# First chunk of an mLSTM cell with a SwiGLU block: how k and q are turned, which engine gates, and in which order weights and gates are asked for

## The chip, the core and the metric

The kernel runs on one core of one Trainium2 chip. The core has five engines that each work through an instruction queue of their own, in order: TensorE (PE in the profile: matrix products, with PEld for its weight loads), VectorE (DVE), ScalarE (ACT), GpSimd (POOL) and SyncE (SP), which here only issues transfers. ScalarE issues some transfers too. Engines wait for each other through semaphores. The metric is the device time of one execution in microseconds, the median of several runs; lower is better.

## The reference

Two blocks follow each other, all in float32 except the three weight matrices, which arrive in float64. The first is an mLSTM cell over a sequence of 768 steps, for 4 batches of 8 heads with 40 features:

```python
for t in range(S):
    m_new = np.maximum(f_gate[:, :, t] + m, i_gate[:, :, t])
    f_stab = np.exp(f_gate[:, :, t] + m - m_new)
    i_stab = np.exp(i_gate[:, :, t] - m_new)
    C = f_stab * C + i_stab * np.einsum('bhd,bhe->bhde', vt, kt)
    n = f_stab * n + i_stab * kt
    h_tilde = np.einsum('bhde,bhe->bhd', C, qt)
    denom = np.maximum(np.abs(np.einsum('bhd,bhd->bh', n, qt)), 1.0)
    y[:, :, t] = 1.0 / (1.0 + np.exp(-o_gate[:, :, t])) * h_tilde / denom
```

Its output, laid out as 3072 tokens of 320 features, goes through a SwiGLU block with 1536 hidden features:

```python
g = x @ w_gate
out = (g / (1.0 + np.exp(-g)) * (x @ w_val)) @ w_out
```

## The kernel before

The sequence is cut into 6 chunks (g = 0 to 5) of 128 steps; a chunk is 512 tokens. Inside a chunk the recurrence is replaced by matrix products: scores of q and k, weighed by exponentials of the gates' running sums and maxima, plus, from chunk 1 on, what comes from the state C. A running sum or maximum is one scan instruction on VectorE. After the cell, `hidden(g, m)` computes block m (of 12) of 128 hidden features for the chunk: 20 products into two PSUM banks (L648), a silu on ScalarE (L653), a product on VectorE (L654). Then the output product follows (L664, or L671 in chunk 0).

TensorE is to run the hidden and output products of all chunks one after the other, and the cell's work for the next chunk is put between them by hand: the lists `slots`, `after` and `first` say after which block which piece of work is issued. Nothing reorders it later: on each engine instructions run in the order in which the program names them. So the order of the calls (L564 to L611, then the loop of L741) is the schedule.

Chunk 0 has no such cover. Its work stands ahead of the first hidden block and is what the change touches. Its steps, for the halves P = 0 and 1 of the 32 batch-head pairs:

- `first_mask`, `first_inputs`, `first_maxima`, `first_exp` (L478 to L495): the weights of the scores, from PSUM through an exponential into `W0`.
- `first_turn` (L504): k and q are transposed on TensorE, 4 products of 128 rows for a bank, two banks for each of k and q in a half; ScalarE and VectorE copy the banks to `kT` and `qT`. Later chunks use `turn_one` (L291), whose products take 64 rows each and fill two banks side by side.
- `first_scores` (L513): scores, then weighing on VectorE (L523).
- `first_own` (L527): 8 products for one batch u, of `W0` with v. `first_x` (L532): four VectorE instructions that divide.
- `sig` (L463): sigmoid of the output gates on ScalarE. `first_gate` (L541): the product with them on VectorE for two batches (L544), then a short copy on GpSimd (L545) that pads x.
- `first_seam` (L555): x is transposed to `xT` on TensorE (L561), three copies out of PSUM.
- `first_state` (L547): 32 products of k and v for the state.
- `late_sums`, `late_maxima`, `late_decay` (L273 to L286): sums, maxima and decays of the gates of all later chunks, on 32 partitions; an exponential on ScalarE (L609) ends them. They are wanted when the gates are turned after block 2 (`late_turns`) and, through the stored `M_dram` (L611), by chunk 1.
- `burn(n)`: n products of no use to the result, which keep TensorE at work.

Weights come in pieces: pieces 0 and 1 hold one block of w_gate and w_val each, pieces 2 to 6 two blocks, pieces 7 to 9 w_out. `piece_load` (L140) issues the gate half on SyncE and the value half (up to piece 4) on ScalarE (both L165). As the weights are float64, each block j goes through `convert(j)`: `scale` (two ScalarE instructions, L190 and L192), `join` (two on VectorE, L199 and L200), `rounded` (one, L207, on GpSimd or VectorE). The intermediate `top` has a single buffer, so the next block's scale waits for the join before. The raw pieces without a `home` share two buffers, so piece 4 waits for the scale of block 0.

PSUM's eight banks are two rings of four, with the tags "cell" and "gen"; a tile takes the next bank of its ring when that is free.

Of the kernel before, what the change touches and what calls it, by code (L numbers as in the profile page):

```python
# [13 lines left out]
AF = mybir.ActivationFunctionType  # L14
# [4 lines left out]
L = 128  # L19
# [5 lines left out]
def kernel(  # L25
# [50 lines left out]
    def bank(name, tag="cell"):  # L76
        return psum.tile([128, 512], F32, name=name, tag=tag)
# [41 lines left out]
    def copy(eng, dst, src):  # L119
        if eng is nc.scalar:  # L120
            nc.scalar.copy(dst, src)
        else:
            eng.tensor_copy(dst, src)
# [16 lines left out]
    def piece_load(p, home=None):  # L140
        kind, m, n = PIECES[p]
        if kind == "gv":
            a, d = NKC, n * 128
            src = [(slice(i * HP, (i + 1) * HP), w[:, m * 128:(m + n) * 128].rearrange("(c p) f -> p c f", p=HP))
                   for i, w in enumerate((moe_w_gate, moe_w_val))]
            queues = (nc.sync, nc.scalar if p < 5 else nc.sync)
        else:
            a, d = n, DM
            src = [(slice(0, 128), moe_w_out[m * 128:(m + n) * 128].rearrange("(a p) d -> p a d", p=128))]
            queues = (nc.sync,)  # L150
        if src[0][1].dtype == F32:
            for r, w in src:
                if kind == "o":
                    nc.sync.dma_start(out=wo_sb[r, m:m + n, :], in_=w)
                else:
                    for x in range(n):
                        nc.sync.dma_start(out=wgv_sb[r, m + x], in_=w[:, :, ts(x, 128)])
            return
        if home is None:
            raw = conv.tile([128, 4 * NKC * 128], U32, name="raw")  # L160
        else:
            raw = home.rearrange("p a t -> p (a t)").bitcast(U32)
        raw = raw[:, 0:2 * a * d]
        for (r, w), queue in zip(src, queues):
            queue.dma_start(out=raw[r].rearrange("p (a d) -> p a d", a=a), in_=w.bitcast(U32))  # L165
        words = raw.rearrange("p (a d two) -> p a d two", two=2, a=a)
        raws[p] = (words[:, :, :, 0], words[:, :, :, 1])
        split(p)
# [16 lines left out]
    def scale(j):  # L185
        if j in blocks:
            lo, hi, dst = blocks[j]
            a, d = hi.shape[1], hi.shape[2]
            top = conv.tile([128, NKC * 128], F32, name="top", bufs=1).rearrange("p (a d) -> p a d", a=a)
            nc.scalar.mul(top, hi.bitcast(F32), 2.0 ** -112)  # L190
            low = conv.tile([128, NKC * 128], I32, name="low").rearrange("p (a d) -> p a d", a=a)
            nc.scalar.mul(low, lo, 2.0 ** -29)  # L192
            blocks[j] = (low, top.bitcast(U32), dst)
# [79 lines left out]
    def late_sums():  # L273
        nc.vector.tensor_tensor_scan(flat(f_sb), flat(keep1), flat(f_sb), 0.0, op0=ALU.mult, op1=ALU.add)
        nc.gpsimd.memset(step1, 0.0)
        nc.gpsimd.tensor_sub(i_sb, i_sb, f_sb)

    def late_maxima():
        nc.vector.tensor_copy(step1[:, 0:1, 0:1], f0[0:BH, end].unsqueeze(1))
        nc.vector.tensor_copy(step1[:, 1:, 0:1], f_sb[:, 0:NL - 1, last])  # L280
        nc.vector.tensor_tensor_scan(flat(M_sb), flat(step1), flat(i_sb), M0[0:BH, end], op0=ALU.add, op1=ALU.max)

    def late_decay():
        nc.vector.tensor_add(m_in[:, 0:1], M0[0:BH, end].unsqueeze(1), f0[0:BH, end].unsqueeze(1))
        nc.vector.tensor_add(m_in[:, 1:], M_sb[:, 0:NL - 1, last], f_sb[:, 0:NL - 1, last])
        nc.vector.tensor_sub(step1, m_in.to_broadcast([BH, NL, SUB]), M_sb)  # L286

    M_dram = tc.dram_tile([BH, S - L], F32, name="M_dram")


# [171 lines left out]
    def sig(P):  # L462
        nc.scalar.activation(o_sb[:, heads(P)], o_sb[:, heads(P)], AF.Sigmoid)  # L463


    def burn(n, tag="cell"):
        t = bank("burn", tag)
        for _ in range(n):
            nc.tensor.matmul(t, lhsT=junk[:, 0:128], rhs=junk, start=True, stop=True)
# [22 lines left out]
    def first_exp(P):  # L492
        for j in range(2):
            for u in (2 * P, 2 * P + 1):
                nc.scalar.activation(W0[:, u * H + j * HH:u * H + (j + 1) * HH], wps[u, j], AF.Exp)  # L495
# [3 lines left out]
    def first_values(P):  # L499
        nc.gpsimd.tensor_copy(w_end[:, heads(P)], W0[:, heads(P), end])  # L500
        nc.gpsimd.tensor_tensor(vw_sb[:, heads(P)], v_sb[:, heads(P)], w_end[:, heads(P)].to_broadcast([128, UH, D1]),
                                op=ALU.mult)

    def first_turn(P, src, dst, engs):  # L504
        for b in range(2):
            tp = bank("tp_kq").rearrange("p (a t) -> p a t", t=L)
            for a in range(UA // 2):
                h = P * UH + b * H + 2 * a
                nc.tensor.transpose(tp[:, a, :], src[:, h:h + 2, :].rearrange("p h d -> p (h d)"), ident)
            a = P * UA + b * UA // 2  # L510
            copy(engs[b], dst[:, a:a + UA // 2, :], tp)

    def first_scores(P):  # L513
        for b in range(2):
            sp = [bank("sp").rearrange("p (a t) -> p a t", t=L) for _ in range(2)]
            a0 = P * UA + b * UA // 2
            for a in range(UA // 2):
                for two in range(2):
                    nc.tensor.matmul(sp[two][:, a, :], lhsT=kT[half(two), a0 + a, :], rhs=qT[half(two), a0 + a, :],
                                     start=True, stop=True)  # L520
            W = W0[:, 2 * a0:2 * a0 + H].rearrange("p (a two) t -> p two a t", two=2)
            for two in range(2):
                nc.vector.tensor_tensor(W[:, two], sp[two], W[:, two], op=ALU.mult)  # L523
# [8 lines left out]
    def first_x(u):  # L532
        y = first_y.pop(u)
        den = work.tile([128, UH, 1], F32, name="den")[:, 0:H]
        nc.vector.tensor_scalar(den, y[:, :, D:], scalar1=1.0, scalar2=None, op0=ALU.max)
        nc.vector.scalar_tensor_tensor(den, in0=y[:, :, D:], scalar=-1.0, in1=den, op0=ALU.mult, op1=ALU.max)
        nc.vector.reciprocal(den, den)
        nc.vector.tensor_tensor(x_sb[:, u, 0:DM].rearrange("p (h d) -> p h d", d=D), y[:, :, 0:D],
                                den.to_broadcast([128, H, D]), op=ALU.mult)

    def first_gate(P):  # L541
        for u in (2 * P, 2 * P + 1):
            x = x_sb[:, u, 0:DM].rearrange("p (h d) -> p h d", d=D)
            nc.vector.tensor_tensor(x, x, o_sb[:, u * H:(u + 1) * H], op=ALU.mult)  # L544
        nc.gpsimd.tensor_copy(x_sb[:, 2 * P:2 * P + 2, DM:], x_sb[:, 2 * P:2 * P + 2, 0:HP])  # L545

    def first_state(P, eng):  # L547
# [7 lines left out]
    def first_seam(P, engs):  # L555
        for c, eng in zip(range(0, NKC, 2), engs):
            cs = range(c, min(c + 2, NKC))
            tp = bank("tp_x")[:, 0:len(cs) * 2 * L].rearrange("p (c u s) -> p c u s", u=2, s=L)
            for w in cs:
                for b in range(2):  # L560
                    nc.tensor.transpose(tp[:, w - c, b, :], x_sb[:, 2 * P + b, ds(PAIRS[w][0] * HP, 2 * HP)], ident)  # L561
            copy(eng, xT(0)[:, c:c + len(cs), 2 * P * L:(2 * P + 2) * L].rearrange("p c (u s) -> p c u s", u=2), tp)
# [3 lines left out]
    for f in (first_mask, first_inputs, first_maxima):  # L566
        for u, j in banks:
            f(u, j)
    first_exp(0)
    first_turn(0, k_sb, kT, (V, V))  # L570
    first_turn(0, q_sb, qT, (A, V))
    first_exp(1)
    first_values(0)
    first_scores(0)
    first_own(0)
    late_sums()
    first_turn(1, k_sb, kT, (A, A))
    first_x(0)
    first_turn(1, q_sb, qT, (A, V))
    load(o_sb, o_gate, 0, 1)  # L580
    piece_load(0)
    piece_load(1)
    late_maxima()
    first_own(1)
    first_values(1)
    first_scores(1)
    first_x(1)
    sig(0)
    sig(1)
    piece_load(2, h_sb[:, NH - NKC:])  # L590
    piece_load(3, wo_sb)
    burn(3)
    first_own(2)
    first_own(3)
    first_gate(0)
    first_x(2)
    first_x(3)
    first_seam(0, (A, A, V))
    scale(0)
    first_gate(1)  # L600
    burn(6, "gen")
    piece_load(4)
    join(0)
    first_seam(1, (A, A, V))
    rounded(0, V)
    first_state(0, A)
    late_decay()
    convert(1)
    nc.scalar.activation(step1, step1, AF.Exp)  # L609
    piece_load(5)  # L610
    nc.sync.dma_start(out=M_dram, in_=flat(M_sb))  # L611

# [127 lines left out]
    }  # L740
    for m in range(NFC):  # L741
        first = [run(convert, j, V if j in on_vector else None) for j in ahead[m]]
        first += {10: [run(scale, 12), run(join, 12)], 11: [run(convert, 13)]}.get(m, [])
        hidden(0, m, first)
        for f in slots.get(m, ()):
            f()
# [99 lines left out]
```

## Time and profile before

| what | us |
|---|---|
| median of 3 runs | 554.64 (554.63 to 554.94) |
| the profiled execution, whole | 555.16 |
| its span, first to last instruction | 553.0 |
| first hidden block starts on TensorE | 31.90 |
| second | 37.45 |
| third | 43.10 |
| TensorE busy in the span | 546.4 |

The span is what the profile shows of an execution; the 2.16 us around it are in the measured time and not in the profile. A line of a timeline gives start, duration, engine (a q behind it: its instruction queue, here an issue of a transfer), line, operation, output and inputs, shapes and count, and in brackets how long the engine had been idle and what ended that. In the chain of waits each line is the start, the duration and the instruction or transfer that the end of the kernel hung on at that time. Lines on a DMA queue give packets, megabytes moved, and the time of the packets as a share of 16 DMA engines; q1 belongs to SyncE, q10 to ScalarE.

### The profile page before, as it was taken

How to read it: one execution, taken by the hardware profiler on the slowest of the kernel's cores; microseconds unless marked ns; L12 is line 12 of the kernel's file. 1: busy time of each engine (PE TensorE's matmuls, PEld its weight loads, DVE VectorE, ACT ScalarE, POOL GpSimd, SP SyncE). 2: the span in 40 equal slices, each digit the busy share in tenths (PEclk: the TensorE clock that was granted, in tenths of full speed). 3: DMA queues.
4: the chain of work that ended last, by engine and by line, in shares of the span. 5: the costliest groups of instructions: out<-in, count | busy, mean ns of one | idle time of the engine just before them, and what ended most of it. 6: DMA issues, size and time to landing. Idle time of an engine off the chain costs nothing.

```text
span 553.0 us, 11595 instructions
## 1 busy us (share of the span) xinstructions
PE 546.4 (99%) x4992; PEld 312.9 (57%) x4992; DVE 234.4 (42%) x394; ACT 134.7 (24%) x202; POOL 106.6 (19%) x97
## 2 busy tenths in 40 slices
PE   8999999999999999999999999999999999999997
PEld 4955546675545575544576455466455567444475
DVE  5956687962156332445521445531426621011100
ACT  4366564443101033110124101005110100111100
POOL 2314355574011151011133001114001200000000
PEclk9999999999999999999999999999999999999999
DMA  9999996798631763660464451395000131000000
GB/s 125 177 280 187 192 274 115 155 111 125 68 49 17 108 109 83 71 76 5 82 127 104 53 68 27 49 149 107 13 1 2 29 62 43 12 1 0 2 24 24
DMA packets 223994, 45.69 MB, mean 83 GB/s; under 512 B 214504, under 2 KB 219112, under 8 KB 223944
## 3 DMA queue, kind: packets, MB, share of 16 engines
q1 hardware_dynamic: 222036, 42.11, 46.7%
q10 hardware_dynamic: 1908, 2.85, 2.0%
q8 instruction: 39, 0.64, 0.5%
q14 instruction: 11, 0.09, 0.1%
HBM read 35.68 MB, written 4.01 MB: 72 GB/s over the span
## 4 chain that ended last, share of the span: by engine, by line
PE 92%; DMA 4%; SPq 3%; POOL 0%; DVE 0%; ACT 0%; issue 0%; ACTq 0%; POOLq 0%
PE gv_ps L648 55%; PE o_ps L664 24%; PE o_ps L671 5%; SPq L117 3%; DMA h_sb<-in_moe_w_val_dram 2%; PE inter L377 2%; PE sp L331 2%; PE intra L382 2%; DMA o_sb<-in_o_gate_dram 2%; PE add L353 1%; PE tp_kq L296 0%; POOL wgv_sb L207 0%; PE tp_x L439 0%; DVE wgv_sb L200 0%; ACT top L190 0%
## 5 line engine op out<-in xcount | busy, mean ns | idle before, releaser
L648 PE MATMUL gv_ps<-xT,wgv_sb 64*128 64x512 f32 x1440 | 317.3, 593 | 1.6 <-POOL wgv_sb L207 1.1
L648 PEld LDWEIGHTS gv_ps<-xT,wgv_sb 64*128 64x128 f32 x1440 | 139.1, 187 | 159.4 <-issue 154.6
L654 DVE TENSOR_TENSOR h_sb<-sg,gv_ps 128x512 f32<-128x512 f32 x72 | 49.5, 687 | 214.5 <-ACT sg L653 214.4
L664 PE MATMUL o_ps<-wo_sb,h_sb 128*128 128x320 f32 x480 | 130.5, 433 | 0.0
L664 PEld LDWEIGHTS o_ps<-wo_sb,h_sb 128*128 128x128 f32 x480 | 90.8, 190 | 41.0 <-issue 3.8
L653 ACT ACTIVATE sg<-gv_ps 128x512 f32<-128x512 f32 x72 | 43.0, 597 | 268.6 <-PE gv_ps L648 268.5
L362 POOL TENSOR_TENSOR C<-C,dec 128x328 f32<-128x328 f32 x20 | 14.5, 735 | 137.7 <-DVE C L369 137.6
L456 POOL TENSOR_SCALAR_AFFINE_SELECT w_sb<-w_sb 64x1024 f32<-64x1024 f32 x20 | 27.8, 1388 | 60.2 <-DVE w_sb L451 59.3
L658 ACT COPY z_sb<-o_ps 128x320 f32<-128x320 f32 x24 | 10.0, 422 | 94.7 <-PE o_ps L664 90.9
L403 POOL TENSOR_TENSOR o_sb<-o_sb,y_sb 128x640 f32<-128x640 f32 x10 | 14.3, 1428 | 79.2 <-DVE y_sb L394 79.1
L671 PE MATMUL o_ps<-wo_sb,h_sb 128*128 128x320 f32 x96 | 26.9, 437 | 0.0
L451 DVE TENSOR_TENSOR w_sb<-g_T,w_sb 128x1024 f32<-128x1024 f32 x10 | 13.2, 1355 | 27.6 <-DMA w_sb<-M_dram 27.6
L426 DVE STREAM_TRANSPOSE xT<-x_sq 128x640 f32<-128x640 f32 x16 | 12.5, 822 | 23.7 <-DMA x_sq<-x_sb 23.7
L671 PEld LDWEIGHTS o_ps<-wo_sb,h_sb 128*128 128x128 f32 x96 | 17.9, 190 | 7.2
L394 DVE TENSOR_TENSOR y_sb<-y_sb,intra 64x328 f32<-64x328 f32 x40 | 19.7, 493 | 0.8 <-PE intra L382 0.2
L369 DVE TENSOR_TENSOR C<-C,add 40x328 f32<-40x328 f32 (+1 forms) x36 | 17.7, 493 | 1.3 <-PE add L353 0.4
L207 POOL TENSOR_TENSOR wgv_sb<-wgv_sb,low 128x640 int32<-128x640 int32 x8 | 12.3, 1541 | 23.7 <-DVE wgv_sb L200 21.9
L377 PEld LDWEIGHTS inter<-C,qT 64*64 64x64 f32 x640 | 10.2, 134 | 7.3 <-issue 6.1
L341 POOL TENSOR_TENSOR vw_sb<-v_sb,w_sb 128x656 f32<-128x656 f32 x10 | 12.8, 1303 | 0.4
L338 DVE TENSOR_TENSOR w_sb<-sp,w_sb 128x512 f32<-128x512 f32 x20 | 12.7, 682 | 0.0
L460 ACT ACTIVATE w_sb<-w_sb 128x1024 f32<-128x1024 f32 x10 | 10.6, 1058 | 8.8 <-POOL w_sb L456 8.8
L397 DVE TENSOR_SCALAR den<-den 128x16 f32<-128x16 f32 x10 | 12.2, 1216 | 0.3
(129 smaller groups left out, 343.7 us busy)
## 6 DMA issues: line engine op xcount, KB each, us to landing
w_sb<-M_dram SPq DMA_DIRECT2D x10, 512.0 KB, 7.2
x_sq<-x_sb SPq DMA_DIRECT2D x128, 40.0 KB, 2.0
k_sb<-in_k_dram SPq DMA_DIRECT2D x12, 320.0 KB, 6.1
v_sb<-in_v_dram SPq DMA_DIRECT2D x12, 320.0 KB, 5.7
o_sb<-in_o_gate_dram SPq DMA_DIRECT2D x12, 320.0 KB, 5.4
raw<-in_moe_w_out_dram SPq DMA_DIRECT2D x3, 1280.0 KB, 7.8
out_dram<-z_sb SPq DMA_DIRECT2D x24, 160.0 KB, 1.8
q_sb<-in_q_dram SPq DMA_DIRECT2D x32, 64.0 KB, 2.4
```

Source lines behind the costliest of these rows:

```text
L117: nc.sync.dma_start(out=dst[:, heads(P), 0:D], in_=tokens(a, c, P))
L362: nc.gpsimd.tensor_tensor(state(s + 1)[:, a], state(s)[:, a], dec[:, s - 2, a].unsqueeze(2).to_broadcast([128, UA, D1]), op=ALU.mult)
L369: nc.vector.tensor_tensor(c, c, ps[r], op=ALU.add)
L377: nc.tensor.matmul(inter[two][half(i), a, :], lhsT=qT[half(two), P * UA + a, half(i)], rhs=state(2 * n + i)[half(two), P * UA + a, :], sta ...
L394: nc.vector.tensor_tensor(t, t, intra[i][half(c)], op=ALU.add)
L403: eng.tensor_tensor(o, o, y[:, :, 0:D], op=ALU.mult)
L456: nc.gpsimd.affine_select(w, w, compare_op=ALU.is_ge, fill=NEG, base=0, pattern=[[0, UH], [1, SUB]], channel_multiplier=-1)
L648: nc.tensor.matmul(ps[i], lhsT=wgv_sb[half(i), m, PAIRS[kc][i] if g < 2 else kc, :], rhs=x[half(i), kc, :], start=(kc == 0), stop=(kc == N ...
L653: nc.scalar.activation(sg, ps[0], AF.Silu)
L654: nc.vector.tensor_tensor(hid(g, m), sg, ps[1], op=ALU.mult)
L664: nc.tensor.matmul(p, lhsT=hid(g, m)[:, ts(u, L)], rhs=wo_sb[:, m, :], start=(m == 0), stop=(m == NFC - 1))
L671: nc.tensor.matmul(ps[u], lhsT=hid(g, m)[:, ts(u, L)], rhs=wo_sb[:, m, :], start=(m == 0), stop=(m == NFC - 1))
```

## The change

In the first chunk `turn_one` takes the place of `first_turn`, which goes. `first_gate` gets an engine for each of its two batches: GpSimd for both of P = 0, VectorE and GpSimd for P = 1. `piece_load(0)` stands ahead of the load of the second output gates (P = 1), `piece_load(1)` behind the first sigmoid. `late_sums` stands ahead of the first exponentials, `late_maxima` behind the first state, ahead of `convert(1)`; `late_decay` follows `convert(1)`, and the exponential that ends these scans (`late_exp`) moves from there into block 0's list, behind `convert(2)` and ahead of its silu. The second batch's division stands ahead of the second scores, `scale(0)` and the second sigmoid ahead of the first seam, and the second burn has 4 products instead of 6.

```diff
@@ -285,6 +285,9 @@
+    def late_exp():
+        nc.scalar.activation(step1, step1, AF.Exp)
+
@@ -501,15 +504,6 @@
-    def first_turn(P, src, dst, engs):
-        for b in range(2):
-            tp = bank("tp_kq").rearrange("p (a t) -> p a t", t=L)
-            for a in range(UA // 2):
-                h = P * UH + b * H + 2 * a
-                nc.tensor.transpose(tp[:, a, :], src[:, h:h + 2, :].rearrange("p h d -> p (h d)"), ident)
-            a = P * UA + b * UA // 2
-            copy(engs[b], dst[:, a:a + UA // 2, :], tp)
-
@@ -538,10 +532,10 @@
-    def first_gate(P):
-        for u in (2 * P, 2 * P + 1):
+    def first_gate(P, engs):
+        for u, eng in zip((2 * P, 2 * P + 1), engs):
             x = x_sb[:, u, 0:DM].rearrange("p (h d) -> p h d", d=D)
-            nc.vector.tensor_tensor(x, x, o_sb[:, u * H:(u + 1) * H], op=ALU.mult)
+            eng.tensor_tensor(x, x, o_sb[:, u * H:(u + 1) * H], op=ALU.mult)
         nc.gpsimd.tensor_copy(x_sb[:, 2 * P:2 * P + 2, DM:], x_sb[:, 2 * P:2 * P + 2, 0:HP])
@@ -566,47 +560,46 @@
+    late_sums()
     first_exp(0)
-    first_turn(0, k_sb, kT, (V, V))
-    first_turn(0, q_sb, qT, (A, V))
+    turn_one(0, k_sb, kT, (V, V))
+    turn_one(0, q_sb, qT, (A, V))
     first_exp(1)
     first_values(0)
     first_scores(0)
     first_own(0)
-    late_sums()
-    first_turn(1, k_sb, kT, (A, A))
+    turn_one(1, k_sb, kT, (A, A))
     first_x(0)
-    first_turn(1, q_sb, qT, (A, V))
+    turn_one(1, q_sb, qT, (A, V))
+    piece_load(0)
     load(o_sb, o_gate, 0, 1)
-    piece_load(0)
-    piece_load(1)
-    late_maxima()
     first_own(1)
     first_values(1)
+    first_x(1)
     first_scores(1)
-    first_x(1)
     sig(0)
-    sig(1)
+    piece_load(1)
     piece_load(2, h_sb[:, NH - NKC:])
     piece_load(3, wo_sb)
     burn(3)
     first_own(2)
     first_own(3)
-    first_gate(0)
+    first_gate(0, (G, G))
     first_x(2)
     first_x(3)
+    scale(0)
+    sig(1)
     first_seam(0, (A, A, V))
-    scale(0)
-    first_gate(1)
-    burn(6, "gen")
+    first_gate(1, (V, G))
+    burn(4, "gen")
     piece_load(4)
     join(0)
     first_seam(1, (A, A, V))
     rounded(0, V)
     first_state(0, A)
+    late_maxima()
+    convert(1)
     late_decay()
-    convert(1)
-    nc.scalar.activation(step1, step1, AF.Exp)
     piece_load(5)
     nc.sync.dma_start(out=M_dram, in_=flat(M_sb))
@@ -740,7 +733,7 @@
-        first += {10: [run(scale, 12), run(join, 12)], 11: [run(convert, 13)]}.get(m, [])
+        first += {0: [run(late_exp)], 10: [run(scale, 12), run(join, 12)], 11: [run(convert, 13)]}.get(m, [])
```

## The prediction, before the changed kernel was run

> **What bounds the kernel now.** I read the page first: TensorE is busy for almost the whole span, and in the chain of waits it owns 92%.
>
> ```profile
> PE 546.4 (99%) x4992; PEld 312.9 (57%) x4992; DVE 234.4 (42%) x394; ACT 134.7 (24%) x202; POOL 106.6 (19%) x97
> ```
>
> So only time before TensorE becomes dense can be won. Where does that begin? The chain of waits in order of time says: at 43.10 us, in the third block of hidden features (m = 2).
>
> ```profile
> 25.43 13.59 DMA h_sb<-in_moe_w_val_dram
> ...
> 39.17 0.81 ACT top L190
> ...
> 41.51 1.54 POOL wgv_sb L207
> ...
> 43.10 4.80 PE gv_ps L648 x20
> ```
>
> From 43.10 to the end it has one hole (0.33 us near 101). The wait that ends last before it is weight piece 2: its value half is asked for at 25.43, because its issue stands behind the second sigmoid, which waited for the second output gates; it lands at 39.02. The TensorE timeline shows what lies ahead of that.
>
> ```profile
> 12.37 2.06 PE L519 MATMUL sp<-qT,kT 64*128 64x128 f32 x32 [0.20 <-ACT qT L121]
> 14.43 0.39 PE L530 MATMUL first_y<-v_sb,h_sb 128*128 128x41 f32 x2
> ...
> 22.88 3.66 PE L530 MATMUL first_y<-v_sb,h_sb 128*128 128x41 f32 x32
> ...
> 31.90 4.56 PE L648 MATMUL gv_ps<-xT,wgv_sb 64*128 64x512 f32 x20 [0.53 <-DVE m_in L285]
> ```
>
> Block 0 starts at 31.90. Block 0, the 32 state products (1.06) and block 1 are 10.12 us, so block 2 could start at 42.02; it starts at 43.10 and then runs 4.80 instead of 4.56, as a bank is freed late. The stall is 1.08 + 0.24 = 1.3 us. Block 0 itself is set by ScalarE's timeline: the split of piece 0 waits for its gate half (landing 28.4), then comes a weight issue on ScalarE's queue, then the copies of xT.
>
> ```profile
> 28.50 0.79 ACT L190 ACTIVATE top<-raw 128x640 f32<-128x640 f32 x1 [0.39 <-DMA raw<-in_moe_w_gate_dram]
> 29.20 0.81 ACT L192 ACTIVATE low<-raw 128x640 int32<-128x640 uint32 x1
> 30.04 0.61 ACTq L165 DMA_DIRECT2D raw<-in_moe_w_val_dram  x1
> 30.69 1.07 ACT L121 COPY xT<-tp_x 128x512 f32<-128x512 f32 x2 [0.68 <-PE tp_x L561]
> ```
>
> VectorE ends its rounding of block 0 at 31.76, the same instant: two chains tie there.
>
> **What the Trainium skill says.** "SBUF — State Buffer", section "SBUF: two separate sides": VectorE and GpSimd share one port pair as an exclusive lock, taken by a VectorE instruction with two SBUF inputs or in a fast mode. The trace agrees: the 0.49 us shift (L199) takes 0.89 where GpSimd's addition runs until 49.92.
>
> ```profile
> 48.37 1.55 POOL L207 TENSOR_TENSOR wgv_sb<-wgv_sb,low 128x640 int32<-128x640 int32 x1 [1.72 <-ACT sg L653]
> ```
> ```profile
> 49.39 0.89 DVE L199 TENSOR_SCALAR wgv_sb<-top 128x640 uint32<-128x640 uint32 x1
> ```
>
> "DMA: Bandwidth & Descriptors", section "Issuing engines are not separate DMA queues": a second issuing queue adds no bandwidth. This trace differs: from 26 to 32 us only SyncE's queue (q1) moves weights, at 196 GB/s, though ScalarE's two issues of 25.4 and 26.1 are pending; from 33 to 38 both move, at 317 GB/s.
>
> ```profile
> q1 hardware_dynamic: 809, 1.17, 109.4%
> ```
> ```profile
> q10 hardware_dynamic: 423, 0.84, 54.3%
> q1 hardware_dynamic: 381, 0.75, 48.6%
> ```
>
> "TensorEngine Tiling (Array Packing)", section "Key Properties": a change of tiling mode drains the array. Here the scores end at 12.37 + 2.06 = 14.43 and one takes 0.27 (278 ns in the groups), so the last starts at 14.16; the next group starts 0.27 later, where the step inside is (2.06 - 0.27) / 16 = 0.11: 0.16 us a change.
>
> **The change part by part.**
>
> *64-row tiles.* The main loop's turn (L296) takes 0.99 us for 32 transposes, so 0.5 for 16; L509 takes 1.07. For the second half that saves 2 x 0.55. But a 64-row pair fills both banks at once. In the first half, bank two is freed by ScalarE's second exponential (10.48) and fourth (11.46), plus 0.18 to TensorE (the first ends at 9.99, TensorE follows at 10.17): k turns 10.66-11.3, VectorE copies to 12.65, q turns 11.64-12.3, and VectorE's q copy ends at 12.60 + 0.69 = 13.3. Each score now needs all four copies, where half of them did before, so scores start at 13.35 instead of 12.37: about 1 us later. Onwards: first_y 15.95 (before 14.98), k and q of the second half from 17.7 to 18.7, with two new mode changes (0.32); the second first_y starts at 18.85 (before 18.42). So TensorE's chain arrives 0.4 late, not early: second scores 20.66, last first_y end 26.98 (before 26.5), VectorE's fourth quotient 28.17 (before 27.89).
>
> *Scans.* late_sums (1.47 on VectorE) goes into its idle 7.4-10.9, after its input landed (issue 1.93 + 5.0); GpSimd's 0.62 + 1.53 follow before 11.5, when it is next wanted. Late_maxima (0.13 + 0.43 + 1.54) leaves the stretch before block 0 and enters that before block 1. Since TensorE sets the pace up to 27 us, both removals only turn into idle time of VectorE there; so does the second quotient's new place ahead of the second scores. The store of M_dram that waits for the maxima stands on SyncE's queue until 38.37 as it is; they end at 34.0.
>
> *Gates.* Three of four 0.48 us gates leave VectorE for GpSimd. 128x328 in 0.735 there (L362) gives 0.72 for 128x320. The first two run at 22.4-23.9, needed at 26.8: hidden. Of the last two, VectorE's comes free at 28.45 and GpSimd's starts at 28.23: the lock costs VectorE between nothing and 0.4 (0.89 - 0.49 above). I take 0.4: gate 29.3. GpSimd's 0.29 pad copy then meets VectorE's join (0.49 + 0.83), nothing to 0.5 more. Join, xT copy (0.42), rounding (0.82) end between 31.3 and 32.2, so block 0 starts at 31.45 to 32.3; I take 32.0. ScalarE has finished piece 0 by then: what was late there isn't any more, and VectorE is late next.
>
> *Weights.* Gate half of piece 0 is issued at 16.64 instead of 19.23 and lands by 24.5; its 1.5 us split is off the path. The second output gates move behind it, from 25.4 to between 26 and 27.3, and the sigmoid (0.74) to 28.0 at worst, just before 28.17, where the last gates want it. ScalarE's halves of pieces 1, 2 and 3 now follow the first sigmoid (21.6): 21.6, 22.2, 22.9, in place of 19.6, 25.4, 26.1. SyncE's gate halves come about 1.5 us later (from 24). Landing of piece 2: if the queues share at some 340 GB/s, 31; if, as between 26 and 32 us in this trace, one queue holds the other up until it is through, 36.5. I take 34.
>
> *Behind block 0.* VectorE: maxima 31.9-34.0, join of block 1 to 35.3, GpSimd's 1.54 to 36.9-37.5; block 1 is due at 32.0 + 4.56 + 1.06 = 37.6. Late_decay (1.1) may be locked by that addition and end at 37.6. Then late_exp, which used to fill ScalarE's 3.66 us wait: now table load 1.28 + 0.74, then 1.28 back to silu, + 0.60 to free the first bank, + 0.75 for the product: 37.6 + 0.74 + 1.28 + 0.60 + 0.75 = 41.0 (its own table is loaded before). Block 2 is due at 32.0 + 10.12 = 42.1. Hidden by 1.1. Block 2's own rounding ends at 40.5. Two burns fewer (2 x 0.22) lie in a wait for the gate.
>
> *Sum.* Dense TensorE begins at 42.1 instead of an effective 43.34 (43.10 + 0.24): -1.2 us. The profiled execution has a span of 553.0 in 555.16, so 551.8 and 553.9; it lies 0.5 above the median 554.64, from which I take the same 1.2: **553.4**.
>
> **Rivals.**
> (A, forecast) Stall gone, block 0 as before: 0.7 to 1.7 us less, 552.9 to 553.9. Chance 0.45.
> (B) The lock doesn't bite in the tail: block 0 at 31.45, dense at 41.55: -1.8, 552.8; if copies come quicker than I assume, 552.2. For it: the ranges of both locks reach zero. Against: GpSimd's gate starts first. Chance 0.2.
> (C) Piece 2 lands at 36.5, piece 1 late too: split ends 38.1, exponential and tables put the product at 42.7, dense at 42.8: -0.5, 554.1. Speaks for it: q10 standing idle from 26 to 32. Chance 0.17.
> (D, slower) late_exp ends up on the path. It sits on ScalarE between the split of piece 2 and the first silu, so with landing at L, bank two is free at L + 1.64 + 2.02 + 1.28 + 0.60 + 0.75 = L + 6.3. It decides from L = 35.8 and loses against before from L = 37.05. If piece 2 lands at 39 as it does now, that is 45.3, +2.0: 556.6. For it: the same bytes queue, and SyncE's half goes later. Against: ScalarE's half is asked for 3 us earlier. Chance 0.18.
>
> That an edit doesn't do what it says is a case for the 64-row turn alone: it shortens the turning and delays what waits for it, which A already counts.
>
> **Numbers.** 0.2% is 1.1 us, about what a measurement here tells from no change: the line is 553.5, through the middle of A. Faster: half of A and all of B, with a little off, 0.43. Same: the other half of A, C and some of D, 0.40. Slower: most of D, 0.17. The range 552.3 to 555.4 leaves out the bottom of B and the upper part of D, under 2 in 10.
>
> **What would show it.** Scores at 13.3; L544 on POOL near 0.72, and VectorE's last gate or the join lengthened beside it; block 0 at 32.0; late_exp after the split of piece 2; no idle before block 2. Wrong if L653's first silu ends after 42, or block 0 starts after 33.

## The result, and the profile after

The changed kernel takes 559.98 us, the median of 20 runs (553.52 to 561.75), and the kernel before 555.48 beside it (554.16 to 558.98, 20 runs). The ratio of the means is 1.0055, with a 95% interval of 1.0028 to 1.0081: slower, by 0.3 to 0.8%, where 0.2% faster was forecast. The changed kernel's times lie in two groups, 7 at 553.5 to 556.9 and 13 at 559.7 to 561.8, with nothing between; the shorter group lies where most executions of the kernel before do. The profiled execution belongs to the second: a span of 559.3 in 561.14.

The chain of waits of the changed kernel, in order of time (start, duration, what), names the loss at once. The product of the hidden blocks is L641 now.

```profile
19.39 17.36 DMA raw<-in_moe_w_gate_dram
...
36.82 0.60 ACTq L165
...
37.47 0.59 ACT xT L121
...
38.11 6.36 PE gv_ps L641 x20
44.47 1.06 PE add L546 x32
45.53 8.78 PE gv_ps L641 x40
```

Block 0 hangs on one weight transfer, the gate half of piece 1, which landed at 36.75. But piece 1 holds the weights of block 1, not of block 0. What carries the wait over is ScalarE's queue, in its timeline:

```profile
27.00 1.07 ACT L121 COPY xT<-tp_x 128x512 f32<-128x512 f32 x2 [0.46 <-PE tp_x L555]
36.82 0.60 ACTq L165 DMA_DIRECT2D raw<-in_moe_w_val_dram  x1
37.47 1.07 ACT L121 COPY xT<-tp_x 128x512 f32<-128x512 f32 x2 [9.39 <-DMA raw<-in_moe_w_gate_dram]
```

The issue of piece 4's value half waits, and the two copies that complete `xT` stand behind it. In the kernel before the same issue went out at 30.04. TensorE, in its timeline, had its transposes done at 30.5 and stood still for 6.54 us, in place of 0.53:

```profile
29.08 1.42 PE L555 MATMUL tp_x<-ident,x_sb 128*128 128x128 f32 x10 [0.60 <-DVE x_sb L538]
30.43 1.13 PE L546 MATMUL add<-vw_sb,k_sb 128*64 128x41 f32 x32
38.11 6.36 PE L641 MATMUL gv_ps<-xT,wgv_sb 64*128 64x512 f32 x20 [6.54 <-ACT xT L121]
```

Block 0 then takes 6.36 where it took 4.56. The page's row of the granted TensorE clock dips in the third of its 40 slices (28 to 42 us; it is 0.50 from 36 to 40):

```profile
PEclk9979999999999999999999999999999999999999
```

So the account of this execution is +6.21 at the start of block 0 (38.11 against 31.90) and +1.80 for its slower products, less the 1.3 that the kernel before lost at block 2 itself and some tenths of overlap where groups meet. Block 2 ends at 54.31 instead of 47.90, +6.41, and the span is 6.3 longer.

Why does that issue wait? Its buffer had been free since the split of piece 0 ended at 25.5. The program's own listing of ScalarE's waits shows a new one, first the kernel before, then the changed one:

```
L165 DMACopy raw<-in_moe_w_val_dram 64x5x512 [waits Activation_49]
L165 DMACopy raw<-in_moe_w_val_dram 64x5x512 [waits DMAHW5_49,Activation_49]
```

This program has eight completion semaphores for its transfers and takes them in turn. A transfer that reuses one must wait until the earlier transfer with it is through. Before, piece 4's value half shared one with piece 0's gate half, which ScalarE had waited for anyway. In the changed kernel the two halves of piece 4 have changed places in the turn: the value half comes one place later, behind the gate half, and gets the semaphore of piece 1's gate half, which has the same one in both kernels. `scale(0)` frees the buffer that both halves wait for. In every kernel here that has it ahead of the first seam the program's listing of transfers shows the gate half first, and in every other the value half. No run moves `scale(0)` alone.

And why did that half land at 36.75, where the same half landed at 30.17 before? Its issue on SyncE was in progress from 19.39 to 23.46. In that time ScalarE, released by the first sigmoid, issued the value halves of pieces 2 and 3 (timelines of SyncE and of ScalarE):

```profile
18.74 0.60 SPq L117 DMA_DIRECT2D o_sb<-in_o_gate_dram  x1
19.39 4.07 SPq L165 DMA_DIRECT2D raw<-in_moe_w_gate_dram  x1
```
```profile
21.21 0.64 ACTq L165 DMA_DIRECT2D h_sb<-in_moe_w_val_dram  x1
22.50 0.60 ACTq L165 DMA_DIRECT2D wo_sb<-in_moe_w_val_dram  x1
```

Of the two queues ScalarE's (q10) then moved nearly all the data from 26 to 30 us, at 205 GB/s in all (packets, MB, share of 16 engines):

```profile
q10 hardware_dynamic: 435, 0.79, 106.4%
q1 hardware_dynamic: 7, 0.01, 1.0%
```

The value halves of pieces 2 and 3 landed at 30.76 and 36.41, the gate halves of pieces 1, 2 and 3 at 36.75, 39.90 and 43.22. From 36 to 42 us it was SyncE's queue alone, at 198 GB/s, where the kernel before had both at work, at 317 from 33 to 38. So the whole stream of loads ran late: `M_dram` was stored at 43.88 instead of 38.37, and the decay weights of chunk 1 (`w_sb`) were asked for at 62.14 instead of 56.61.

These are two suspects: Q, the wait in ScalarE's queue, and S, the order in which transfers are served, which also makes the stream late. A third is C, the edits to the computing.

### The profile page after: what moved, and what is told of

It reads as the page before. It is cut to its first block, busy times and chain, and to the rows that moved or that the text cites. A ratio compares the mean times of both kernels' runs of the same rounds, so it can differ in the third digit from the quotient of the medians.

```text
span 559.3 us, 11660 instructions
## 1 busy us (share of the span) xinstructions
PE 545.9 (98%) x5022; PEld 310.1 (55%) x5022; DVE 233.8 (42%) x391; ACT 134.4 (24%) x202; POOL 107.9 (19%) x100
## 4 chain that ended last, share of the span: by engine, by line
PE 93%; SPq 3%; DMA 3%; ACT 0%; issue 0%; ACTq 0%
PE gv_ps L641 57%; PE o_ps L657 23%; PE o_ps L664 5%; DMA raw<-in_moe_w_gate_dram 3%; SPq L117 3%; PE inter L380 2%; PE sp L334 2%; PE intra L385 2%; PE add L356 1%; PE tp_kq L299 0%; SPq L165 0%; PE tp_x L442 0%; PE add L546 0%; SPq L132 0%; PE tp_g L615 0%
## 5 line engine op out<-in xcount | busy, mean ns | idle before, releaser
L641 PE MATMUL gv_ps<-xT,wgv_sb 64*128 64x512 f32 x1440 | 318.6, 596 | 6.5 <-ACT xT L121 6.5
L641 PEld LDWEIGHTS gv_ps<-xT,wgv_sb 64*128 64x128 f32 x1440 | 137.6, 188 | 167.1 <-issue 158.5
```

What stands on the lines that cost most here:

```text
L641: nc.tensor.matmul(ps[i], lhsT=wgv_sb[half(i), m, PAIRS[kc][i] if g < 2 else kc, :], rhs=x[half(i), kc, :], start=(kc == 0), stop=(kc == N ...
```

## The experiments

Each kernel ran beside the kernel before on the same chip. Line numbers move a little from kernel to kernel.

**Take the wait out of ScalarE's queue.** The changed kernel, with piece 4's value half on SyncE:

```diff
-            queues = (nc.sync, nc.scalar if p < 5 else nc.sync)
+            queues = (nc.sync, nc.scalar if p < 4 else nc.sync)
```

> The changed kernel with one edit: the value half of weight piece 4 is issued on SyncE instead of ScalarE. Theory Q (queue): in the changed kernel ScalarE's issue of that half waited until 36.75 us for the landing of piece 1's gate half, whose completion semaphore it reuses, and the xT copies stood behind it. Without it block 0 starts at 32 us instead of 38.1. Piece 1's gate half still lands late (about 36.7), so block 1 waits for its conversion and starts near 40.6 (due 37.6), and block 2, behind the moved exponential, near 46 instead of 50: 556 us, some 4 below the changed kernel. Theory B (bytes: the late gate half itself holds everything): no change, block 0 near 38. Theory C (the compute edits cost it): no change.

559.96 us against 554.98, ratio 1.0084 (1.0052 to 1.0116). The mechanism was right: block 0 starts at 31.91, so the edits to the computing cost nothing there. The time was not. TensorE's timeline:

```profile
31.91 4.56 PE L641 MATMUL gv_ps<-xT,wgv_sb 64*128 64x512 f32 x20 [0.28 <-DVE keep L280]
...
39.95 4.56 PE L641 MATMUL gv_ps<-xT,wgv_sb 64*128 64x512 f32 x20 [2.42 <-POOL wgv_sb L207]
44.96 5.18 PE L641 MATMUL gv_ps<-xT,wgv_sb 64*128 64x512 f32 x20 [0.44 <-ACT sg L646]
...
82.03 6.25 PE L641 MATMUL gv_ps<-xT,wgv_sb 64*128 64x512 f32 x18 [1.59 <-DVE h_sb L647]
```

After 45 us it is more than 4 us ahead of the changed kernel, and at 90 us level with it (90.23 against 90.00). VectorE's timeline says where the gain went:

```profile
76.40 1.22 DVE L454 TENSOR_TENSOR w_sb<-g_T,w_sb 128x1024 f32<-128x1024 f32 x1 [4.49 <-DMA w_sb<-M_dram]
```

The same instruction started at 70.97 in the kernel before, after a wait of 1.31. The late stream of loads comes to the surface here, 45 us after its cause: VectorE waits for `w_sb` with the products of the hidden blocks queued behind. In the changed kernel the instruction starts at 75.99 with no wait at all. There the computing is as late as the data, and the second loss is hidden behind the first. That piece 4's value half now burdens SyncE adds little: `w_sb` was asked for at 62.49, in the changed kernel at 62.14.

Of the 4.4 us lost between 70 and 90 us, 1.7 are slower products behind the wait: the 18 from 82.03 took 6.25 where loads_only, behind a wait at the same place, took 4.56, and the granted clock was 0.50 from 84 to 86 us. Two of the six executions, with a mean granted clock of 1.000, took 557.6 and 557.9; the other four, at 0.994 to 0.997, took 559.3 to 562.0. By these two, 2.6 to 2.9 us of this kernel's loss come without a fallen clock.

**Give piece 1's gate half its place back.** The changed kernel, with pieces 2 and 3 asked for behind the second sigmoid:

```diff
-    piece_load(2, h_sb[:, NH - NKC:])
-    piece_load(3, wo_sb)
...
     sig(1)
+    piece_load(2, h_sb[:, NH - NKC:])
+    piece_load(3, wo_sb)
```

> The changed kernel with the value halves of pieces 2 and 3 issued behind the second sigmoid, as before the change, all else as changed. Theory Q with theory S (service: ScalarE's three value halves are served ahead of piece 1's gate half): piece 1's gate half lands near 28 to 30 instead of 36.7, block 0 starts at 32, and there is no wait in ScalarE's queue. Piece 2's value half lands near 38 to 39 as before, so the moved exponential is exposed: block 2 at 44.5 to 45.5 against an effective 43.3 before: 556 to 557 us. Theory B without S: gate half late anyway, near 560. Theory C: near 560.

556.75 us against 554.98, ratio 1.0033 (1.0019 to 1.0047). The gate half landed at 29.85 and ScalarE's issue went out at 29.93, in time for the copies of `xT` (block 0 at 33.70; in this execution the work ahead of it was about 1 us later, and the granted clock was 0.50 from 28 to 30 us); and `w_sb` was asked for at 57.71. Most of the loss is gone with an edit that changes only when two transfers are asked for. Block 2 took 5.19 behind the exponential of the late gates (piece 2's value half landed at 38.4).

**The edits to the computing alone.** The loads, `sig` and `scale(0)` in the order of the kernel before:

```diff
-    piece_load(0)
     load(o_sb, o_gate, 0, 1)
+    piece_load(0)
+    piece_load(1)
...
     sig(0)
-    piece_load(1)
+    sig(1)
...
-    scale(0)
-    sig(1)
     first_seam(0, (A, A, V))
+    scale(0)
```

> The kernel before with the compute edits alone (64-row turns, gates on GpSimd, scans and exponential moved, 4 burns); all loads, sigmoids and the first scale where they were before. Theory Q: no transfer is overtaken, block 0 starts at 31.9 to 32.3; piece 2 lands at 39.0 and the moved exponential with its two table loads puts block 2 near 45.3 instead of an effective 43.3: plus 2.0, 557 us. Theory C: the compute edits carry the loss, 560 us, block 0 near 38.

555.13 us, ratio 0.9998 (0.9982 to 1.0013): no difference that can be told, where 557 was expected. The exponential was exposed as rival D of the prediction has it: piece 2 landed at 37.73, and ScalarE's timeline runs from its split through the exponential,

```profile
37.89 0.78 ACT L190 ACTIVATE top<-h_sb 128x640 f32<-128x640 f32 x1 [4.06 <-DMA h_sb<-in_moe_w_val_dram]
...
39.38 1.28 ACT L289 ACT_TABLE_LOAD   x1
40.67 0.74 ACT L289 ACTIVATE keep<-keep 32x640 f32<-32x640 f32 x1
```

so that block 2 starts at 43.46 and takes 5.18. That is 0.74 behind the kernel before (43.10 and 4.80), and it is 0.74 behind at 90 us too (90.83 against 90.09), but at the start of chunk 1's blocks only 0.39 (127.78 against 127.39).

**The edits to the loads alone.** The same diff the other way round, on the kernel before:

```diff
-    load(o_sb, o_gate, 0, 1)
     piece_load(0)
-    piece_load(1)
+    load(o_sb, o_gate, 0, 1)
...
     sig(0)
-    sig(1)
+    piece_load(1)
...
+    scale(0)
+    sig(1)
     first_seam(0, (A, A, V))
-    scale(0)
```

> The kernel before with the edits of the loads alone (piece 0 ahead of the second output gates, pieces 1 to 3 behind the first sigmoid, second sigmoid and first scale ahead of the first seam); turns, gates, scans and burns as before. Theory Q: the wait of ScalarE's queue is here in full, block 0 near 38, dense near 49: 559 to 561 us in most executions. Theory C: 553 to 555 us.

559.64 us, ratio 1.0091 (1.0060 to 1.0121). The loads carry the whole loss. ScalarE's timeline repeats that of the changed kernel, 2 us earlier because the gate half landed at 34.58:

```profile
34.65 0.60 ACTq L165 DMA_DIRECT2D raw<-in_moe_w_val_dram  x1
35.30 1.07 ACT L121 COPY xT<-tp_x 128x512 f32<-128x512 f32 x2 [5.86 <-DMA raw<-in_moe_w_gate_dram]
```

**Does the wait follow the semaphore?** The changed kernel with one transfer more, of 32 values that nothing uses, ahead of piece 4:

```diff
     burn(4, "gen")
+    for t in range(1):
+        nc.sync.dma_start(out=warm[t * BH:(t + 1) * BH], in_=gate_rows(f_gate)[:, t:t + 1])
     piece_load(4)
```

> The changed kernel with one more load on SyncE, 32 values of 4 bytes into a tile that nothing reads any more, programmed ahead of piece 4. It moves every later transfer one place on in the turn of completion semaphores: the value half of piece 4 now shares one with the gate half of piece 2 instead of that of piece 1, and the value halves of pieces 2 and 3 come to wait for piece 0's gate half and for the second output gates. Theory Q (ScalarE's issue waits for the transfer that used its completion semaphore before): ScalarE's issue of piece 4 ends at the landing of piece 2's gate half, within 0.1 us of it and not of piece 1's, the two copies to xT follow within 1 us, and block 0 starts 1.3 us after that landing. Rival (the issue waits for its buffer, or for ScalarE's own conversion): the issue comes before 31 us and block 0 starts at 32 to 33, whatever piece 2 does. Theory S is neutral here, but says that piece 3's value half, now behind the output gates' landing at about 26 us, no longer overtakes piece 1's gate half, which lands by 32.5 instead of 36.75.

It does. Piece 2's gate half landed at 34.42, and ScalarE's timeline names it, a transfer into another buffer for another block:

```profile
34.49 0.60 ACTq L165 DMA_DIRECT2D raw<-in_moe_w_val_dram  x1
35.14 1.07 ACT L121 COPY xT<-tp_x 128x512 f32<-128x512 f32 x2 [5.81 <-DMA h_sb<-in_moe_w_gate_dram]
```

Block 0 started at 35.78, 1.36 after the landing. S was right too: piece 3's value half went out at 25.37, and piece 1's gate half landed at 29.54. The one execution took 559.56. Here the stream of loads was nearly cured (`w_sb` asked for at 58.69) and the wait kept, and the loss is still some 4.6 us, 2.8 of them in the products of block 0, which took 7.39 in place of 4.56. With the first experiment this makes a pair: either fault alone, with its slower products, costs nearly what both cost together.

**The changed kernel again.** Unchanged, for an execution of its shorter group.

> The changed kernel itself once more, one look, to see an execution of its shorter group of times (7 of its 20 times lay at 553.5 to 556.9 us, 13 at 559.7 to 561.8). Theory S says that the two groups differ in whether the value halves of pieces 2 and 3 are accepted ahead of piece 1's gate half. If this execution ends by 557, piece 1's gate half lands by 33 us, ScalarE's issue of piece 4 is done by 33 and block 0 starts by 34.5. If it ends at 559 or later, the gate half lands at 34 to 37 again, block 0 starts 1.3 us after it. An execution below 557 with the gate half landing after 35, or one above 559 with it landing before 32, would be against it.

It took 560.09, so what the shorter executions do differently was not seen. In this one the gate half landed at 35.26 and block 0 started at 36.62, as expected of the longer group. Over eight executions, of seven kernels, the landing of piece 1's gate half falls into two classes by one comparison, whether its issue on SyncE was finished when ScalarE issued piece 2's value half:

| kernel | gate half of piece 1: issue ends | value half of piece 2: issue begins | gate half lands |
|---|---|---|---|
| before | 22.89 | 25.43 | 30.17 |
| compute_only | 21.24 | 25.00 | 30.16 |
| late_values | 22.35 | 26.59 | 29.85 |
| one_tiny_load | 22.21 | 22.79 | 29.54 |
| loads_only | 21.97 | 21.30 | 34.58 |
| changed_again | 22.76 | 21.52 | 35.26 |
| p4_on_sync | 24.03 | 22.00 | 35.94 |
| the changed kernel | 23.46 | 21.21 | 36.75 |

In the six kernels below, which are not in the table, the issue ends first too, and the half lands at 28.92 to 30.16.

**Can a better order win?** Two attempts to bring piece 2 forward, by asking for piece 3 behind piece 4: once on compute_only, once on the kernel before.

```diff
-    piece_load(3, wo_sb)
...
     piece_load(4)
+    piece_load(3, wo_sb)
```

> The kernel with the change's compute edits and the load order of the kernel before (compute_only), with piece 3 asked for behind piece 4 instead of ahead of it. Theory S (transfers of the two queues are served in the order in which they were accepted, and a value half is late because of the gate half accepted ahead of it): without piece 3's gate half in front of it the value half of piece 2 lands by 34.5 us instead of 37.73, block 2 is no longer held back by its weights or by the exponential and starts at 42.2 to 42.5; 553.9 us where the kernel before takes 555.0, ratio 0.998. Rival (the rate of the queue itself makes piece 2's value half late, the order doesn't matter): it lands after 37 and the ratio stays at 1.000. A third outcome: piece 3, later by about 1 us, holds back block 4, and the ratio is 1.000 or above with a wait before block 4.

> The kernel before with nothing changed but piece 3, asked for behind piece 4. Theory S: piece 2's value half lands by 34.5 us instead of 39.02, the 1.2 us that block 2 loses to its late weights in the kernel before are gone, block 2 starts at 42.0 to 42.3: 553.8 us where the kernel before takes 555.0, ratio 0.998. Rival: the value half lands after 37 us in any order, ratio 1.000. If the whole stream of weights is what ends late, and not the order in it, the gain is given back behind 70 us at the weights of the second chunk, and the ratio is 1.000 with an earlier block 2.

557.22 us, ratio 1.0042 (1.0028 to 1.0056), and 556.93, ratio 1.0040 (1.0027 to 1.0053): both slower, in the manner of the last branch of the second expectation. Piece 2's value half landed at about 36.8 and 36.6, earlier than in compute_only (37.73) and the kernel before (39.02), but not by 34.5, as theory S had it. Block 2 did start earlier: at 42.52 on compute_only, and on the kernel before without any gap behind block 1. But the later loads paid: `w_sb` was asked for at 58.07 and 57.71 instead of 56.61, and VectorE, in the timeline of the second, waits for it longer than in the kernel before:

```profile
71.98 1.23 DVE L451 TENSOR_TENSOR w_sb<-g_T,w_sb 128x1024 f32<-128x1024 f32 x1 [4.25 <-DMA w_sb<-M_dram]
```

**The exponential back at its old place**, on compute_only:

```diff
     late_decay()
+    late_exp()
...
-        first += {0: [run(late_exp)], 10: [run(scale, 12), run(join, 12)], 11: [run(convert, 13)]}.get(m, [])
+        first += {10: [run(scale, 12), run(join, 12)], 11: [run(convert, 13)]}.get(m, [])
```

> compute_only with the late exponential put back ahead of block 0 (behind late_decay), so that its two table loads and itself no longer stand on ScalarE between piece 2's conversion and block 0's own activations. If the exponential at its new place costs what the chain from piece 2's landing suggests, about 0.7 us, this is 554.4 us where compute_only is at 555.1, ratio to the kernel before 0.9987. If the exponential is hidden at either place, the ratio is that of compute_only, 0.9998. If its table loads ahead of block 0 delay the copies to xT, block 0 starts later than 32 us and the ratio is above 1.001.

555.15 us, ratio 1.0004 (0.9995 to 1.0014). Blocks 1 and 2 now run without a gap, and the last block of chunk 0 starts at 89.13, 1.70 earlier than in compute_only and 0.96 earlier than in the kernel before. Chunk 1's blocks start at 127.89, against 127.78 and 127.39. The exponential's new place costs its 1.7 us, then, but in a stretch where a microsecond won is not kept: VectorE waits 2.16 for `w_sb` at 70.49 already, and what is left goes before 128.

**Where does it go?** In the kernel before VectorE waits 2.81 us at 125.78 for the 32-row loads of k for chunk 2. Three kernels ask for them ahead of v and the output gates, the first based on the kernel before and the others on exp_at_old_place; the last also has `weights_load(1)` ahead of piece 6:

```diff
-        1: [run(do_gather, 1, 1), run(weights_load, 2), run(load_all, v_sb, v, 2)],
+        1: [run(do_gather, 1, 1), run(weights_load, 2), run(early_squares, 0), run(load_all, v_sb, v, 2)],
...
-        3: [run(do_divide, 1, 1), run(load_all, o_sb, o_gate, 2), run(early_squares, 0)],
+        3: [run(do_divide, 1, 1), run(load_all, o_sb, o_gate, 2)],
```

> The kernel before with the 32-row loads of k for the third chunk asked for ahead of v and the output gates of that chunk, not behind them. In the kernel before VectorE waits 2.81 us for these loads at 125.78, and every later chunk runs to a fixed pattern from there. If the order of SyncE's loads is what paces this stretch, they land by 119 us, the wait is gone and the kernel takes 552 to 553 where the kernel before takes 555, ratio 0.995. If the wait only hides one for v or the output gates, now later by 10 us, the ratio is 1.000 or above. The change's own edits play no part.

> The kernel with the change's compute edits, the load order of the kernel before and the exponential at its old place (exp_at_old_place), with the 32-row loads of k for the third chunk ahead of v and the output gates. In exp_at_old_place block 9 began 1 us earlier than in the kernel before (89.13 against 90.09) and the gain was gone at 128 us, where VectorE waited 2.69 us for these loads. If that wait is what takes the gain, this is another 1 us shorter than the kernel before with the same edit: 551 to 552.5, ratio 0.994. If the compute edits give nothing at any place, it stands where the kernel before with the same edit stands, within 0.2%.

> compute_squares_first with the decay weights of the second chunk also asked for ahead of piece 6, one block earlier. VectorE waits 2.16 us for these weights at 70.49 in exp_at_old_place (1.31 at 70.97 in the kernel before). If SyncE's order paces this stretch too, they land 3 us earlier and the wait goes, another 0.5 to 2 us: 550 to 552, ratio 0.992. If piece 6, later by as much, is what block 10 or 11 then waits for, or the loads behind 80 us end where they did, nothing is gained on compute_squares_first.

All three lost at least as much as the change does: ratios 1.0087 (1.0061 to 1.0114), 1.0091 (1.0072 to 1.0110) and 1.0089 (1.0068 to 1.0111). The wait for k went. The sigmoid of the output gates started 8 us later instead (124.40 against 116.25), and ScalarE's timeline (kernel before with this edit alone) shows the queue of the main finding a second time, with a sigmoid in place of the issue:

```profile
124.40 0.74 ACT L463 ACTIVATE o_sb<-o_sb 128x640 f32<-128x640 f32 x1 [8.84 <-DMA o_sb<-in_o_gate_dram]
126.28 0.74 ACT L463 ACTIVATE o_sb<-o_sb 128x640 f32<-128x640 f32 x1 [1.14 <-DMA o_sb<-in_o_gate_dram]
127.03 1.28 ACT L460 ACT_TABLE_LOAD   x1
128.33 2.00 ACT L460 ACTIVATE w_sb<-w_sb 128x1024 f32<-128x1024 f32 x2
130.24 0.73 ACT L658 COPY z_sb<-o_ps 128x320 f32<-128x320 f32 x2
```

The exponentials and the copies that free the output product's banks stand behind the sigmoid, and chunk 1's blocks start at 130.69 instead of 127.39. No kernel tried here is faster than the kernel before; compute_only and exp_at_old_place equal it. Which wait paces 90 to 128 us there is not settled: taking away one only showed another behind it.

## Why the prediction was wrong

The forecast was 553.4. The step that failed is in the paragraph on the gates, where the sum takes block 0 at 32.0: "ScalarE has finished piece 0 by then: what was late there isn't any more, and VectorE is late next." ScalarE had finished piece 0, at 25.5. But ahead of the last copies of `xT` its queue holds the issue of piece 4, and that got a new wait, on a transfer of no concern to block 0. The prediction's own quotation from the kernel before shows this order: issue at 30.04, then copies of `xT`. The sum gives that issue no wait: of what piece 4 waits for, only its buffer had been considered, and not its completion semaphore. Block 0 started at 38.11, past the 33 that the prediction names as a sign of being wrong. This one wait makes +6.2, and the slower products behind it +1.8.

The second failure is in the paragraph on the weights. It named the right trace (q10 standing idle from 26 to 32 us) and, as one of two cases, what then happened (one queue holds the other up until it is through), and applied it to one side only. It asked when piece 2's value half would land, 31 to 36.5; that half landed at 30.76. It did not ask what the three value halves, now first, would do to the gate halves that "come about 1.5 us later": they came 6.6, 6.5 and 5.5 us later, and piece 2 was whole only at 39.90. Rival C says "piece 1 late too" and prices only block 2. Nothing in the sum followed the stream of loads past block 2, to `w_sb` at 71 us; p4_on_sync shows that the late stream brings a loss of 5.0 us without the wait in ScalarE's queue, part of it as slower products.

The other steps, against the profile:

- 64-row turns. Scores start 3.10 after the first k turn (9.78 to 12.88), 0.90 more than the 2.20 before: about 1 us, as forecast. As that turn itself started 0.4 earlier, the scores came at 12.88 (13.35 forecast). By the last first_y, which ends at 26.5 in both kernels, nothing is left of it; 0.4 was forecast.
- Scans. Moved at no cost that can be told, as forecast: compute_only is at 0.9998.
- Gates. GpSimd's took 0.85 and 0.86, not 0.72. The lock made VectorE's gate 1.02 instead of 0.48, +0.54 where 0.4 was taken:

```profile
28.00 1.02 DVE L538 TENSOR_TENSOR x_sb<-x_sb,o_sb 128x320 f32<-128x320 f32 x1
```
```profile
27.81 0.86 POOL L538 TENSOR_TENSOR x_sb<-x_sb,o_sb 128x320 f32<-128x320 f32 x1 [4.20 <-DVE x_sb L532]
```

  The gate ends at 29.02 (29.3 forecast), VectorE's rounding of block 0 at 31.70 (31.3 to 32.2). Where piece 4's issue holds nothing up block 0 starts at 31.91 (p4_on_sync) and 32.26 (compute_only): the 32.0 was right for the computing.
- Piece 0 and the output gates. The gate half of piece 0 landed at 22.42 (by 24.5) and the second output gates at 25.78 (26 to 27.3).
- late_exp, "hidden by 1.1". In the changed kernel block 0 is so late that nothing of it shows. Where block 0 is on time it was not hidden: compute_only against exp_at_old_place prices it at 1.7 us at the last block of chunk 0. That is rival D, right as a mechanism: with piece 2 at 37.73 its L + 6.3 gives the end of VectorE's product at 44.0, and it ended at 44.04. Yet D's reckoning that this reaches the end did not hold (0.9998 against 1.0004, intervals that overlap). The same goes for the forecast gain itself, the stall ahead of block 2: exp_at_old_place and before_piece3_behind_4 remove it, and neither is faster.

So the sum failed twice over. Its 1.2 us could be won at block 2 but not kept, and the loss came from a queue and a stream of loads that it had not followed.

## What to carry to other kernels

When a load, or the work that frees its buffer, is moved, write out the order of all transfers on all queues, find for each issue the earlier transfer whose completion semaphore it reuses, and look at what stands behind that issue on its engine. An engine that both computes and issues transfers stakes its computing on every transfer that its issues wait for. Then follow the moved bytes to the last load that stands behind them, and not only to the first that is needed: a late stream can surface 45 us later, and a gain ahead of such a point may not be kept.

## What was not expected of the hardware

- Two queues took turns. Where one queue's transfers were accepted first, the other stood still for 4 to 6 us at a time, and all 16 DMA engines together moved 194 to 205 GB/s (28 to 32 us before; 26 to 30 and 36 to 42 after). Where both moved, they had 317. The Trainium skill ("DMA: Bandwidth & Descriptors", section "Issuing engines are not separate DMA queues") expects no gain of a second issuing queue; these traces differ, before and after the change alike. Why the second queue starts when it does was not isolated.
- The granted clock of TensorE fell to 0.50 for 3.4 or 6.8 us at a time, in nine of the fourteen traces, and a pause is no full account of it. After 6.54 us idle, block 0 took 6.36 instead of 4.56, and in one_tiny_load 7.39 after 3.66; in p4_on_sync products were slow after only 1.59 us idle. After 2.49 us idle (loads_only) block 0 took 4.56 as ever. And in late_values, where TensorE was busy for all of the 4 us from 24 to 28, the clock fell at 27, and ten transposes took 2.38 where they took 1.29 in the changed kernel (row of the clock, and TensorE's timeline of late_values). What makes it fall is not shown.

```profile
PEclk9989999999999999999999999999999999999999
```
```profile
27.65 2.38 PE L555 MATMUL tp_x<-ident,x_sb 128*128 128x128 f32 x10
```

- The lock between VectorE and GpSimd doubles more than a gate: `late_decay`'s subtraction took 2.19 beside GpSimd's addition of 1.54 (timelines of VectorE and GpSimd of the changed kernel), where it took 0.81 in the kernel before.

```profile
41.11 2.19 DVE L286 TENSOR_TENSOR keep<-m_in,M_sb 32x640 f32<-32x640 f32 x1
```
```profile
41.08 1.54 POOL L207 TENSOR_TENSOR wgv_sb<-wgv_sb,low 128x640 int32<-128x640 int32 x1 [11.51 <-DVE m_in L285]
```

- Two groups of times of one kernel, 553.5 to 556.9 and 559.7 to 561.8. Only the longer group was seen in a profile. The mean granted clock recorded with each execution is 0.993 to 0.997 in the longer and 0.996 to 1.000 in the shorter, so a fallen clock goes with the longer times, but as the ranges meet it is not all of the difference. That in the shorter one piece 1's gate half wins the race for acceptance is a guess that fits the table above; it is not shown.
